# RWKV-5 attention with a two-layer feed-forward: three transposes given to transposing DMAs

## The chip, the core and the metric

The kernel runs on one core of one Trainium2 chip. The metric is the device time in microseconds (us). Before the change it is 203.04 us, the median of three runs (202.64 to 203.18). A profile is one execution of the program, recorded by the hardware profiler.

## What is computed

The reference first runs a recurrent attention over 4 batches, 8 heads, 768 time steps and a head width of 48, and then a feed-forward on its output:

```python
for t in range(S):
    cur = einsum('bhd,bhe->bhde', u * k[t], v[t])
    y[t] = einsum('bhd,bhde->bhe', r[t], state + cur)
    state = w * state + einsum('bhd,bhe->bhde', k[t], v[t])
x = y.transpose(0, 2, 1, 3).reshape(B * S, H * D)       # 3072 x 384
h = x @ w_in                                            # 384 x 2048
g = where(h >= 1, h, where(h <= -1, 0, (h + 1) ** 2 / 4))
out = g @ w_out                                         # 2048 x 384
```

Inputs and output are float32.

## The kernel before

The recurrence is cut into 6 chunks of 128 time steps. Inside a chunk it becomes matmuls: R and K are scaled by powers of w that depend on the row (tiles `Rs` and `Ks`, bf16), the scaled products of all pairs of steps form a 128 x 128 matrix A per head, a mask keeps the earlier steps, and the chunk's sum over K and V updates a state per batch.

A *unit* is one chunk of one batch (128 rows, all 8 heads); a *group* is two units, that is one chunk of two batches. There are 12 groups (0 to 11) and 24 units. Heads are taken in pairs: each head's 48 columns are padded to 64, so a pair fills 128 columns, and a unit has NP = 4 pairs.

For a unit, the stages are these functions:

- `att0` (lines 214 to 224): eight TensorE transposes (tile `T` in PSUM, line 221), four of the unit's scaled R and four of its scaled K, and one VectorE copy to `TT` in SBUF (line 223).
- `att1` (226 to 236): eight matmuls for A from `TT` (line 232), masked by VectorE into `AT` (line 235, two instructions).
- `att2` (238 to 272): `Sp`, the state's sum, from the untransposed `Ks` and V (line 247); `Y` from `TT` with the state (line 254) and from `AT` with V (line 259); VectorE forms `Tm` (266) or the first state (269), and `y` (271), to which it adds the term with u, `V2`.
- `att3` (287 to 295): three TensorE transposes of `y` (tile `X`, line 292).
- `att4` (297 to 299): a ScalarE copy of `X` into half of `xT`, the group's input to the feed-forward.
- `decay` (GpSimd, line 279) and `new_state` (ScalarE, line 285) bring the state forward.

For a group, `load_rk` (lines 77 to 80) issues one DMA for R and one for K on the SP queue, and `load_v` (84) one for V on GpSimd's queue. Both have 48-element runs, 192 bytes in DRAM. `product` (180 to 197) has four GpSimd multiplications: 0 makes `Rs` (line 191), 1 makes `Ks` (193), 2 `KU` (195), 3 `RKU` (197). `u_sums` (VectorE, line 201, tile `diag`) sums RKU, and `u_term` (GpSimd, line 206) makes `V2`. For group 0 the work is split by unit, and VectorE makes its `Rs` and `Ks`. There are three buffers each for R, K, `Rs` and `Ks`, five for V and two for y.

The feed-forward of a group has four quarters. `mm1` (310) is 12 matmuls into `hp` (PSUM, two buffers); `act` is two ScalarE instructions, `pt` (321) and `sq` (323); `act_end` is one VectorE instruction, `gt` (329). `mm2` (341) takes eight of the 16 matmuls of a unit's output into `op` (PSUM, one buffer); after the second half ScalarE copies `op` to `o_sb` (347, two buffers) and SP stores it (349).

The order is written out by hand: every engine and every DMA queue takes its instructions in the order in which the program names them, and an instruction that waits holds up all behind it on its engine. The loop over steps t, four steps per group, is what sets that order. Which stage falls in which step comes from the offsets in these lines:

```python
at_a, at_b, at_1, at_2, at_p = at(0), at(2), at(L1), at(L2), at(-4)   # L1, L2 = 7, 11
at_e = at(L1 + 1)
```

So for group g: `att0` and `att1` of its two units at steps 4g to 4g+3; `att2` and `att3` (with `att4`) at 4g+2 to 4g+5; `mm1` at 4g+7 to 4g+10; `act_end` one step later; `mm2` at 4g+11 to 4g+14; the four products at 4g-4 to 4g-1. Inside a step the order is: `att0` or `att1`; the loads of R and K of the group two ahead (in steps that divide by four, from step 4 on) and of V; `act_end`; `mm1` and `act`; `att2` or `att3`; the product; `u_sums` and `u_term`; `mm2` with its store. R and K of groups 0, 1 and 2 are issued ahead of the loop. The weights `w_in` (two DMAs, line 93, ahead of the loop) and `w_out` (two DMAs, line 97, step 3) are loaded on GpSimd's queue.

Of the kernel before, what the change touches and what calls it, by code (L numbers as in the profile page):

```python
# [9 lines left out]
BF16 = mybir.dt.bfloat16  # L10
# [4 lines left out]
P = 128  # L15
# [3 lines left out]
UNITS = 2  # L19
# [3 lines left out]
def kernel(  # L23
# [11 lines left out]
    nc = tc.nc  # L35
    B, H, S, D = r.shape
    NCH = S // C
    NP = H // 2
# [3 lines left out]
    nK = DM // P  # L42
# [10 lines left out]
    att = ctx.enter_context(tc.tile_pool(name="att", bufs=2))  # L53
# [3 lines left out]
    ps1 = ctx.enter_context(tc.tile_pool(name="ps1", bufs=1, space=bass.MemoryType.PSUM))  # L57
# [8 lines left out]
    def load_tiles(g):  # L66
        R = loads.tile([P, UNITS * H, D], F32, name="R", tag="R")
        K = loads.tile([P, UNITS * H, D], F32, name="K", tag="K")
        V = loads.tile([P, UNITS * H, D], BF16, name="V", tag="V", bufs=5)
        loaded[g] = (R, K, V)  # L70
# [6 lines left out]
    def load_rk(g, j0=0, j1=UNITS):  # L77
        R, K, V = loaded[g]
        nc.sync.dma_start(out=R[:, j0 * H : j1 * H, :], in_=source(r, g, j0, j1))  # L79
        nc.sync.dma_start(out=K[:, j0 * H : j1 * H, :], in_=source(k, g, j0, j1))  # L80

    def load_v(g, j0=0, j1=UNITS):
        V = loaded[g][2]
        nc.gpsimd.dma_start(out=V[:, j0 * H : j1 * H, :], in_=source(v, g, j0, j1))  # L84
# [33 lines left out]
    for j in range(UNITS):  # L118
# [13 lines left out]
    ident = const.tile([P, P], BF16, name="ident")  # L132
# [4 lines left out]
        out=umask, in_=umask, compare_op=ALU.is_ge, fill=1.0,  # L137
# [12 lines left out]
    states_bf = [const.tile([P, NP, 2 * D], BF16, name="state_bf", tag=f"sb{b}") for b in range(B)]  # L150
# [9 lines left out]
    for j in range(2):  # L160
        rows = slice(j * HP, j * HP + D)
# [8 lines left out]
    ready = {}  # L170
# [9 lines left out]
    def product(g, i, eng=None, j0=0, j1=UNITS):  # L180
        eng = eng or nc.gpsimd
        R, K, V, R_s, K_s, KU, RKU, diag, V2 = ready[g]

        def part(x):
            return x.rearrange("p (b h) d -> p b h d", b=UNITS)[:, j0:j1]

        def rep(x):
            return x.unsqueeze(1).to_broadcast([P, j1 - j0, H, D])

        if i == 0:  # L190
            eng.tensor_mul(part(R_s)[:, :, :, :D], part(R), rep(Wup))  # L191
        elif i == 1:
            eng.tensor_mul(part(K_s)[:, :, :, :D], part(K), rep(Wdn))  # L193
        elif i == 2:
            eng.tensor_mul(part(KU), part(K), rep(u_row))  # L195
        else:
            eng.tensor_mul(part(RKU), part(R), part(KU))  # L197

    def u_sums(g, j0=0, j1=UNITS):
        hs = slice(j0 * H, j1 * H)  # L200
        nc.vector.tensor_reduce(ready[g][7][:, hs], ready[g][6][:, hs, :], AX.X, ALU.add)  # L201

    def u_term(g, eng, j0=0, j1=UNITS):
        hs = slice(j0 * H, j1 * H)
        V, diag, V2 = ready[g][2], ready[g][7], ready[g][8]
        eng.tensor_mul(  # L206
            V2[:, hs, :], V[:, hs, :], diag[:, hs].unsqueeze(2).to_broadcast([P, (j1 - j0) * H, D])
        )


    unit = {}
    xT = {}

    def att0(n):
        g, j = divmod(n, UNITS)
        R_s, K_s = ready[g][3:5]
        T = ps1.tile([P, 2 * NP, P], BF16, name="T", tag="a")
        for i, x in enumerate((R_s, K_s)):
            for p in range(NP):
                h = j * H + 2 * p  # L220
                nc.tensor.transpose(T[:, i * NP + p, :], x[:, h : h + 2, :].rearrange("p h d -> p (h d)"), ident)  # L221
        TT = att.tile([P, 2 * NP, P], BF16, name="TT", tag="TT")
        nc.vector.tensor_copy(TT, T)  # L223
        unit[n] = [TT, None, None]

    def att1(n):
        TT = unit[n][0]
        A2 = [ps1.tile([P, NP, P], F32, name=f"A{j}", tag="ab"[j]) for j in range(2)]
        for p in range(NP):
            for j in range(2):  # L230
                rows = slice(j * HP, j * HP + D)
                nc.tensor.matmul(A2[j][:, p, :], TT[rows, NP + p, :], TT[rows, p, :], start=True, stop=True)  # L232
        AT = att.tile([P, 2, NP, P], BF16, name="AT", tag="AT")
        for j in range(2):
            nc.vector.tensor_mul(AT[:, j], A2[j], umask.unsqueeze(1).to_broadcast([P, NP, P]))  # L235
        unit[n][1] = AT

    def att2(n):
        g, j = divmod(n, UNITS)
        c, b = g // BP, (g % BP) * UNITS + j  # L240
        V, K_s, V2 = ready[g][2], ready[g][4], ready[g][8]
        TT, AT, _ = unit[n]
        if c + 1 < NCH:
            Sp = ps1.tile([P, NP, 2 * D], F32, name="Sp", tag="b")
            for p in range(NP):
                h = j * H + 2 * p
                nc.tensor.matmul(  # L247
                    Sp[:, p, :], K_s[:, h : h + 2, :].rearrange("p h d -> p (h d)"),
                    V[:, h : h + 2, :].rearrange("p h d -> p (h d)"), start=True, stop=True,
                )  # L250
        Y = ps1.tile([P, H, D], F32, name="Y", tag="y")
        for p in range(NP):
            if c:
                nc.tensor.matmul(  # L254
                    Y[:, 2 * p : 2 * p + 2, :].rearrange("p h d -> p (h d)"), TT[:, p, :], states_bf[b][:, p, :],
                    start=True, stop=False, skip_group_check=True,
                )
            for i in range(2):
                nc.tensor.matmul(  # L259
                    Y[:, 2 * p + i, :], AT[:, i, p, :], V[:, j * H + 2 * p + i, :],  # L260
                    start=(c == 0), stop=True, skip_group_check=True,
                )
        if c + 1 < NCH:
            if c:
                Tm = att.tile([P, NP, 2 * D], F32, name="Tm", tag="Tm")
                nc.vector.tensor_add(Tm, Sp, states[b])
                decays[n] = Tm
            else:
                nc.vector.tensor_mul(states[b], Sp, wCm)
        y = att.tile([P, DM], BF16, name="y", tag="y")  # L270
        nc.vector.tensor_add(y, Y.rearrange("p h d -> p (h d)"), V2[:, j * H : (j + 1) * H, :].rearrange("p h d -> p (h d)"))
        unit[n][2] = y
# [14 lines left out]
    def att3(n):  # L287
        g, j = divmod(n, UNITS)
        y = unit.pop(n)[2]
        X = ps1.tile([P, nK, P], BF16, name="X", tag="y")  # L290
        for i in range(nK):
            nc.tensor.transpose(X[:, i, :], y[:, i * P : (i + 1) * P], ident)  # L292
        if j == 0:
            xT[g] = moe.tile([P, nK, TOK], BF16, name="xT", tag="xT", bufs=3)
        unit[n] = X

    def att4(n):
        g, j = divmod(n, UNITS)
        nc.scalar.copy(xT[g][:, :, j * P : (j + 1) * P], unit.pop(n))  # L299


    gs = {}
# [76 lines left out]
    for t in range(N):  # L379
        for n, odd in [(g * UNITS + i // 2, i % 2) for g, i in at_a.get(t, ())]:  # L380
            att1(n) if odd else att0(n)
            if n == 0:
                if odd:
                    u_sums(0, 0, 1)
                    u_term(0, nc.vector, 0, 1)
                else:
                    product(0, 0, nc.vector, 1, 2)
                    product(0, 1, nc.vector, 1, 2)
        if t % nQ == 0 and 3 <= t // nQ + 2 < nG:
            g = t // nQ + 2  # L390
            load_tiles(g)
            load_rk(g)
        if t % nQ == 1 and t // nQ + 2 < nG:
            load_v(t // nQ + 2)
        if t == 3:
            load_w_out(0)
            load_w_out(1)
        for g, q in at_e.get(t, ()):
            act_end(g, q)
        for g, q in at_1.get(t, ()):  # L400
            mm1(g, q)
            act(g, q)
        for n, odd in [(g * UNITS + i // 2, i % 2) for g, i in at_b.get(t, ())]:
            att3(n) if odd else att2(n)
            if odd:
                att4(n)
                decay(n)
            elif n:
                new_state(n - 1)
        if t == 2:  # L410
            u_sums(0, 1, 2)
            u_term(0, nc.vector, 1, 2)
        for g, i in at_p.get(t, ()):
            if g:
                if i == 0:
                    prepare_tiles(g)
                product(g, i)
        if t % nQ == 0 and 0 < t // nQ < nG:
            u_sums(t // nQ)
            u_term(t // nQ, nc.gpsimd)  # L420
        for g, i in at_2.get(t, ()):
            mm2(g, i)
# [30 lines left out]
```

## Time and profile before

| | |
|---|---|
| median of three runs | 203.04 us |
| the profiled execution | 203.65 us |
| its span, first to last instruction | 201.9 us |
| busy: TensorE, VectorE, ScalarE, GpSimd | 171.6, 140.3, 140.5, 134.3 us |
| granted TensorE clock | 1.00 throughout |
| T on TensorE (line 221), 192 matmuls | 10.3 + 10.5 us |
| TT on VectorE (line 223), 24 copies | 16.6 us, 690 ns each |
| X on TensorE (line 292), 72 matmuls | 8.5 us |
| xT on ScalarE (line 299), 24 copies | 11.0 us, 460 ns each |
| SP queue (R, K, u, out) | 53168 packets, 14.36 MB, 34.6% of 16 engines |
| GpSimd queue (V, weights, w) | 27712 packets, 5.51 MB, 31.4% |

How to read it. The profile gives, for each engine, the time in which it was busy, and the span in 40 slices in which a digit is the busy share in tenths. Its *chain of waits* starts at the last instruction and goes back, at each step, to what released it; a line's share of that chain says how much of the span it held up. Groups of instructions are named by source line, engine, and what they write and read; "hp<-xT,w_in_sb" is the matmul that writes `hp`. Matmuls overlap in the pipeline, so the mean of one (278 ns for `mm1`) is longer than the distance between two; the chain shows the latter. "SPq" is the SP engine's issuing of DMAs; how long after its issue a transfer has landed is shown apart from that. SP's instructions are not counted as busy.

### The profile page before, as it was taken

What the parts mean: (1) busy time and instruction counts of PE and PEld (TensorE: products, weight loads), DVE (VectorE), ACT (ScalarE), POOL (GpSimd) and SP (SyncE); (2) the same over time, 40 slices, a digit from 0 to 9 for tenths busy, and PEclk for the clock granted to TensorE, in tenths of its full rate; (3) what the DMA queues carried; (4) which work ended last, traced back from release to release, by engine and by line L of the source; (5) the groups of instructions that cost most, each with busy time, mean ns of one, the idle gap of its engine ahead of it and who ended that gap; (6) DMA issues with size and microseconds to landing.
All of it is one profiled execution on the core that took longest, in us unless ns stands there. A gap on an engine that the chain in (4) does not pass through costs nothing.

```text
span 201.9 us, 4347 instructions
## 1 busy us (share of the span) xinstructions
PE 171.6 (85%) x1768; PEld 129.3 (64%) x1768; DVE 140.3 (70%) x197; ACT 140.5 (70%) x173; POOL 134.3 (67%) x102
## 2 busy tenths in 40 slices
PE   0045419979999999999999999999999999999782
PEld 0023317767778777877787778777877786777541
DVE  3189636598968888869688888697787876543320
ACT  4511010789887878787878787878788878898810
POOL 7079999989798796996996969969969020000000
PEclk9999999999999999999999999999999999999999
DMA  5999999999978278836873785568110111101121
GB/s 110 171 212 187 202 135 172 182 158 174 173 45 177 63 64 171 77 82 128 67 152 85 42 196 65 76 136 81 39 40 4 39 42 39 42 0 41 39 78 42
DMA packets 81044, 20.34 MB, mean 101 GB/s; under 512 B 74880, under 2 KB 80256, under 8 KB 81024
## 3 DMA queue, kind: packets, MB, share of 16 engines
q1 hardware_dynamic: 53168, 14.36, 34.6%
q0 software_dynamic: 27712, 5.51, 31.4%
q8 instruction: 14, 0.23, 0.5%
q10 hardware_dynamic: 144, 0.20, 0.5%
q14 instruction: 6, 0.05, 0.1%
HBM read 20.84 MB, written 4.72 MB: 127 GB/s over the span
## 4 chain that ended last, share of the span: by engine, by line
PE 75%; POOL 8%; DVE 4%; DMA 3%; ACT 3%; issue 3%; SPq 2%; POOLq 0%; ACTq 0%
PE hp L310 31%; PE op L341 29%; PE T L221 5%; PE A L232 3%; DMA u_bc<-in_u_dram 3%; PE Y L259 2%; POOL KU L195 2%; PE X L292 2%; POOL RKU L197 2%; PE Y L254 2%; ACT pt L321 2%; SPq L79 2%; PE Sp L247 1%; ACT o_sb L347 1%; POOL V L84 1%
## 5 line engine op out<-in xcount | busy, mean ns | idle before, releaser
L321 ACT ACTIVATE pt<-hp,half_col 128x1024 f32<-128x1024 f32 x48 | 53.4, 1113 | 31.6 <-PE hp L310 31.3
L310 PE MATMUL hp<-xT,w_in_sb 128*128 128x256 bf16 x576 | 72.9, 278 | 1.1 <-DVE gt L329 1.1
L341 PE MATMUL op<-w_out_sb,gt 128*128 128x384 bf16 x384 | 69.9, 326 | 2.3 <-ACT o_sb L347 2.0
L329 DVE SCALAR_TENSOR_TENSOR gt<-sq,hp 128x1024 bf16<-128x1024 f32 x48 | 58.2, 1213 | 12.5 <-ACT sq L323 12.5
L310 PEld LDWEIGHTS <-w_in_sb 128*128 128x128 bf16 x576 | 54.8, 99 | 10.7 <-issue 1.4
L323 ACT ACTIVATE sq<-pt,zero_col 128x1024 f32<-128x1024 f32 x48 | 55.2, 1149 | 1.6
L341 PEld LDWEIGHTS <-gt 128*128 128x128 bf16 x384 | 35.2, 97 | 22.3 <-issue 3.1
L235 DVE TENSOR_TENSOR AT<-A,umask 128x512 bf16<-128x512 f32 x48 | 30.8, 683 | 7.4 <-PE A L232 7.2
L223 DVE COPY TT<-T 128x1024 bf16<-128x1024 bf16 x24 | 16.6, 690 | 21.8 <-PE T L221 21.8
L206 POOL TENSOR_TENSOR V<-V,diag 128x768 f32<-128x768 bf16 x11 | 16.2, 1474 | 20.6 <-DVE diag L201 20.3
L221 PE MATMUL T<-ident,Rs 128*128 128x128 bf16 x96 | 10.3, 237 | 18.7 <-DVE Rs L191 10.1
L195 POOL TENSOR_TENSOR KU<-K,u_bc 128x768 f32<-128x768 f32 (+1 forms) x13 | 22.0, 1689 | 6.4 <-DMA u_bc<-in_u_dram 6.4
L197 POOL TENSOR_TENSOR RKU<-R,KU 128x768 f32<-128x768 f32 (+1 forms) x13 | 22.1, 1700 | 0.3
L221 PEld LDWEIGHTS <-Rs 128*128 128x128 bf16 x96 | 8.0, 106 | 21.6 <-DVE Rs L191 10.6
L299 ACT COPY xT<-X 128x384 bf16<-128x384 bf16 x24 | 11.0, 460 | 14.3 <-PE X L292 14.3
L193 POOL TENSOR_TENSOR Ks<-K,Wdn 128x768 bf16<-128x768 f32 x11 | 20.0, 1817 | 0.0
L191 POOL TENSOR_TENSOR Rs<-R,Wup 128x768 bf16<-128x768 f32 x11 | 19.9, 1813 | 0.0
L279 POOL TENSOR_TENSOR state<-Tm,wCm 128x384 f32<-128x384 f32 x16 | 16.0, 1002 | 0.1
L347 ACT COPY o_sb<-op 128x384 f32<-128x384 f32 x24 | 11.2, 467 | 5.7 <-PE op L341 5.7
L232 PE MATMUL A<-TT 48*128 48x128 bf16 x192 | 11.6, 232 | 3.4 <-DVE TT L223 2.0
L84 POOL DMA_DIRECT2D V<-in_v_dram x12 | 14.4, 1202 | 0.0
L201 DVE TENSOR_REDUCE diag<-RKU 128x16 f32<-128x768 f32 (+1 forms) x13 | 11.5, 881 | 3.1 <-POOL RKU L197 3.1
(48 smaller groups left out, 145.8 us busy)
## 6 DMA issues: line engine op xcount, KB each, us to landing
out_dram<-o_sb SPq DMA_DIRECT2D x24, 192.0 KB, 1.9
R<-in_r_dram SPq DMA_DIRECT2D x11, 384.0 KB, 4.4
K<-in_k_dram SPq DMA_DIRECT2D x11, 384.0 KB, 6.0
V<-in_v_dram POOLq DMA_DIRECT2D x12, 192.0 KB, 5.0
w_in_sb<-in_moe_w_in_dram POOLq DMA_DIRECT2D x2, 768.0 KB, 9.0
w_out_sb<-in_moe_w_out_dram POOLq DMA_DIRECT2D x2, 768.0 KB, 17.1
R<-in_r_dram SPq DMA_DIRECT2D x2, 192.0 KB, 6.0
K<-in_k_dram SPq DMA_DIRECT2D x2, 192.0 KB, 5.4
```

The source lines that it names most:

```text
L191: eng.tensor_mul(part(R_s)[:, :, :, :D], part(R), rep(Wup))
L193: eng.tensor_mul(part(K_s)[:, :, :, :D], part(K), rep(Wdn))
L195: eng.tensor_mul(part(KU), part(K), rep(u_row))
L197: eng.tensor_mul(part(RKU), part(R), part(KU))
L221: nc.tensor.transpose(T[:, i * NP + p, :], x[:, h : h + 2, :].rearrange("p h d -> p (h d)"), ident)
L232: nc.tensor.matmul(A2[j][:, p, :], TT[rows, NP + p, :], TT[rows, p, :], start=True, stop=True)
L235: nc.vector.tensor_mul(AT[:, j], A2[j], umask.unsqueeze(1).to_broadcast([P, NP, P]))
L310: nc.tensor.matmul(hp[:, f, :], w_in_sb[:, i, n0 : n0 + P], xT[g][:, i, :], start=(i == 0), stop=(i == nK - 1), skip_group_check=True,)
L321: nc.scalar.activation(pt, hp, AF.Relu, bias=half_col, scale=0.5)
L323: nc.scalar.activation(sq, pt, AF.Square, bias=zero_col)
L329: nc.vector.scalar_tensor_tensor(out=gt, in0=sq, scalar=1.0, in1=hp, op0=ALU.min, op1=ALU.max)
L341: nc.tensor.matmul(o_ps[g], gs[g, q][:, f, j * P : (j + 1) * P], w_out_sb[:, n, :], start=(n == 0), stop=(n == nF - 1),)
```

## The change

All transposes but those of group 0's R and K leave TensorE. A new function, `transpose_in`, issues one transposing DMA on SP for a group's whole `Rs` (128 x 1024) or `Ks`, right behind the product that makes it, in the steps 4g-4 and 4g-3. Its result, `RT` or `KT`, has three buffers. `att0` is left with nothing to issue for groups 1 to 11, and takes the unit's half of these tiles. `att3` issues one transposing DMA on SP for a unit's y (128 x 384), straight into its half of `xT`, and `att4` is gone, with the ScalarE copy. In `att1` and `att2`, `TT[0]` is the transposed R and `TT[1]` the transposed K.

```diff
+    scaled_T = {}
+
+    def transpose_in(g, i):
+        x = ready[g][3 + i].rearrange("p h d -> p (h d)")
+        t = att.tile([P, UNITS * NP, P], BF16, name="TT"[:1] + "RK"[i], tag="RK"[i] + "T", bufs=3)
+        nc.sync.dma_start_transpose(out=t, in_=x)
+        scaled_T[g, i] = t
+
     def att0(n):
         g, j = divmod(n, UNITS)
+        if g:
+            cols = slice(j * NP, (j + 1) * NP)
+            unit[n] = [[scaled_T[g, i][:, cols, :] for i in range(2)], None, None]
+            return
...
-        unit[n] = [TT, None, None]
+        unit[n] = [[TT[:, :NP, :], TT[:, NP:, :]], None, None]
...
-                nc.tensor.matmul(A2[j][:, p, :], TT[rows, NP + p, :], TT[rows, p, :], start=True, stop=True)
+                nc.tensor.matmul(A2[j][:, p, :], TT[1][rows, p, :], TT[0][rows, p, :], start=True, stop=True)
...
     def att3(n):
         g, j = divmod(n, UNITS)
         y = unit.pop(n)[2]
-        X = ps1.tile([P, nK, P], BF16, name="X", tag="y")
-        for i in range(nK):
-            nc.tensor.transpose(X[:, i, :], y[:, i * P : (i + 1) * P], ident)
         if j == 0:
             xT[g] = moe.tile([P, nK, TOK], BF16, name="xT", tag="xT", bufs=3)
-        unit[n] = X
-
-    def att4(n):
-        g, j = divmod(n, UNITS)
-        nc.scalar.copy(xT[g][:, :, j * P : (j + 1) * P], unit.pop(n))
+        nc.sync.dma_start_transpose(out=xT[g][:, :, j * P : (j + 1) * P], in_=y)
...
             if odd:
-                att4(n)
                 decay(n)
...
                 product(g, i)
+                if i < 2:
+                    transpose_in(g, i)
```

More of the change, by code (lines that the diff above doesn't have):

```diff
@@ L254, in att2 @@
                 nc.tensor.matmul(
-                    Y[:, 2 * p : 2 * p + 2, :].rearrange("p h d -> p (h d)"), TT[:, p, :], states_bf[b][:, p, :],
+                    Y[:, 2 * p : 2 * p + 2, :].rearrange("p h d -> p (h d)"), TT[0][:, p, :], states_bf[b][:, p, :],
                     start=True, stop=False, skip_group_check=True,
```

## The prediction

> **What bounds the kernel now.** I read the page's slices and chain first, then the chain in order of time in the middle, then the SP queue's timeline at the start.
>
> ```profile
> PE   0045419979999999999999999999999999999782
> ...
> DMA  5999999999978278836873785568110111101121
> ...
> PE hp L310 31%; PE op L341 29%; PE T L221 5%; PE A L232 3%; DMA u_bc<-in_u_dram 3%; PE Y L259 2%; POOL KU L195 2%; PE X L292 2%; POOL RKU L197 2%; PE Y L254 2%; ACT pt L321 2%; SPq L79 2%; PE Sp L247 1%; ACT o_sb L347 1%; POOL V L84 1%
> ```
>
> A slice is 5.05 us. There are three stages. To about 45 us TensorE is idle or half busy, while the DMA row reads 9 up to 60 us. From 45 to 171 us TensorE is full. After 171 us TensorE and ScalarE take turns. The chain's T (5%) and X (2%) are the transposes that the change takes away. The middle of the chain, in order of time (start, us, what):
>
> ```profile
> 97.23 1.31 PE hp L310 x12
> 98.54 0.17 PE Sp L247 x4
> ...
> 99.08 1.30 PE op L341 x8
> 100.38 0.33 PE A L232 x8
> 100.71 1.42 PE hp L310 x12
> 102.12 0.17 PE X L292 x3
> 102.29 1.30 PE op L341 x8
> 103.59 0.45 PE T L221 x8
> 104.04 1.31 PE hp L310 x12
> ```
>
> Two steps of the loop take 6.81 us (97.23 to 104.04) without a gap, and all of it is TensorE. The SP queue at the start (start, us in the queue's issue):
>
> ```profile
> 12.74 1.49 SPq L80 DMA_DIRECT2D K<-in_k_dram  x1
> 16.59 1.97 SPq L79 DMA_DIRECT2D R<-in_r_dram  x1
> 18.66 9.11 SPq L80 DMA_DIRECT2D K<-in_k_dram  x1
> 28.67 5.18 SPq L79 DMA_DIRECT2D R<-in_r_dram  x1
> 33.94 9.40 SPq L80 DMA_DIRECT2D K<-in_k_dram  x1
> 43.43 4.23 SPq L79 DMA_DIRECT2D R<-in_r_dram  x1
> 47.71 4.43 SPq L80 DMA_DIRECT2D K<-in_k_dram  x1
> 53.99 0.36 SPq L349 DMA_DIRECT2D out_dram<-o_sb  x1
> ```
>
> These are K of group 2, R and K of groups 3, 4, 5, and the first store. By the tile view of K and R in narrow windows, K2 lands 14.9 us after its issue (at 27.6), R3 15.5 (32.1), K3 24.7 (43.4), R4 19.2 (47.9), K4 18.0 (51.9). An issue's end coincides with a landing: K3's with K2's (27.8, 27.6), K4's with K3's (43.3, 43.4), R5's with R4's (47.7, 47.9). So SP gets about two loads ahead and then waits for the oldest, and the loads land in the order of issue. The start is bound by this queue.
>
> **The middle: what is removed.** T is 0.45 us every second step; it lies on the chain from 49.10 to 164.55, so 18 times: 8.1 us. X is 0.17 us in each other step from 47.63 on, 20 times: 3.4 us. Together 11.5 us, and two steps become 6.19 us. What is late next: VectorE needs per two steps 2 x 1.21 (gt) + 2 x 0.68 (AT) + 0.55 (y) + 0.55 (Tm) + half of 0.94 (diag) = 5.4 us (the 0.69 of TT goes); ScalarE 2 x 2.26 + 0.47 + 0.50 = 5.5 us (the 0.46 of xT goes); GpSimd per four steps 4 x 1.81 + 1.47 + 1.20 + 2 x 1.00 = 11.9 against 12.4 us. All still fit. Closest is the hp buffer, of which there are two: hp started at 97.06, its gt ended at 103.16 behind AT, so the hp two steps later can't start before 6.15 to 6.2 us. That may take back 0 to 1 us; I take 11.0 for the middle.
>
> **The middle: what is added.** Per group SP issues two transposes of 128x1024 and two of 128x384, and each waits in SP's order for its source. No DMA of this kind is in the trace. *SP's time for it*: between 0.36 us (an unhindered store) and the 1.41 us that K's issue has as its median; I take 1 to 1.5, as it has half of a load's pieces but is another instruction. That makes 4 to 6 us, beside 1.8 for the loads and 0.7 for the stores, of 12.4. *The engines' time*: a load is 2048 pieces of 192 B; a transpose reads 1024 (384 for y) rows of 256 B. In the undisturbed middle K lands 1.55 us behind R (R's landing 3.9 us, K's 5.0, issued 0.45 later), 0.76 ns a piece. At that price a group's 2816 rows take 2.1 us; the nearest lower bound is nothing, the upper one I set at twice the price per row. The DMA share was 0.68 between 60 and 100 us, 9.3 us in a group of 13.62; 9.3 + 2.1 to 4.2 us against 12.4 may meet the bound of one full set of engines, but shares up to 1.58 are in the trace (40 to 50 us), so I cost it at nothing.
>
> The 128x1024 results have cover: Rs is ready in the step of its product (105.88 in the group around 104) and read five steps later; Ks ends at 113.19 and is read three to four steps later. For y: the late half is ready at 106.83; SP is held by the store until 108.84; with 1 us of issue and some 2 to 3 us to land (a store takes 1.9) it is there at 112, and the hp that reads it starts two steps on, at 114.3. The cover is 2 us; if a y transpose took 5.5 us, each further us would cost one per group, 11 in all. Behind a transpose that waits on SP stand only stores and loads: o_sb has two buffers and two steps a store (6 us), the loads are four steps ahead.
>
> The Trainium skill speaks against the change here. "VectorE: DVE Perf Modes", section The three transpose paths, gives 1309 ns for a 128x128 transpose by DMA and 390 ns on TensorE, and its rules say to use TensorE where PSUM will do. Eight T took 0.45 us in this trace, 56 ns each, so the page's TensorE figure isn't what this kernel pays. By the page's DMA figure, an estimate, 22 blocks a group would take 29 us and the kernel some 190 us more. [...]
>
> **The start: what is moved.** Here I expect the change to lose. SP's order becomes: ... K2; R' and K' of group 1 (steps 0, 1; a dash marks a transpose); y' of unit 0 (step 3); R3, K3 (step 4); R'2 (step 4, behind the loads in the code); y' of unit 1 (step 5). The first mm1 needs both y' and started at 33.05. Now SP waits for Rs of group 1 (GpSimd, ends 20.32) and for Ks (23.28), so R3's issue moves from 16.59 to about 26, and y' of unit 1 stands behind K3, which landed at 43.4 even when it was issued early.
>
> The queue from K2's landing at 27.6 holds, up to that y': 1024 + 1024 + 384 + 2048 (R3) + 2048 (K3) + 1024 + 384 = 7936 rows or pieces. R3 and K3 together landed in 15.8 us (27.6 to 43.4), 260 a us, beside w_out, whose second half lands at 45.2 (25.9 + 19.3); afterwards R4 and K4 landed in 8.5 us, 480 a us. So 17.6 us x 260 = 4580 by 45.2, and the other 3360 in 7.0 us: 52.2. The V load of step 5 is gone at 48.9 (32.2 + 16.7), after which it is faster: 50.3 if the last 1500 go at 0.76 ns. I take **51** for the first mm1. Ends: 44 if the transposes cost the queue nothing, 60 if a row costs twice a piece.
>
> From the first mm1 to the first mm2 it was 33.1 to 47.8, 14.7 us, a stretch set by VectorE (gt, AT, diag one behind the other); one TT of 0.6 us goes: 14.1. Nothing there catches up: GpSimd's u_term waits for diag, which stands behind the first gt. Then 201.9 - 47.8 = 154.1 us, less 11.0. The tail keeps its turns: the last xT copy ended at 178.36; y is ready at 173.75 and 4 us by DMA gives the same. Sum: 51 + 14.1 + 143.1 = 208.2 us of span, 6.3 above 201.9. The execution took 203.65, 1.75 above its span and 0.6 above the median of 203.04. On the median: 203.04 + 6.3 = **209.3 us**.
>
> **Rivals.**
> - *The start loses more than the middle gains* (forecast): first mm1 between 46 and 60, 204 to 218 us. Chance 0.55.
> - *Transposes nearly free for the queue*: first mm1 at 44 to 46, 201.5 to 204. For it: no HBM is read. Against: loads ahead remain. 0.13.
> - *The transposes do not stand behind the loads' pieces* (the faster side): another path lets y' of unit 1 pass R3 and K3. SP still issues it behind K3, whose issue would end when K2 has landed (27.8), then R'2 after Rs at 30.4, y' at about 31.5, landed by 34 to 36. The middle's 11 us remain: 191.5 to 196. It decides as soon as y' lands before 44. For it: loads and weights on two queues did pass each other. Against: SP's own loads land strictly in order. 0.19.
> - *Slow transposes*: above about 3.7 ns a row (five times a piece) a group's 10.4 us and the other 9.3 pass 1.58 x 12.4, and the engines bind the middle; at twice that, about 19 us a group for some 8 groups, 55 us more. 218 to 270. For it: a transpose splits its rows over 128 partitions, and no row shows its price. 0.13.
>
> **Numbers.** About 0.3% (0.6 us) can be told from no change. Faster: 0.19 and 0.05 of the second; same 0.05; slower 0.71. The range reaches from the upper end of the third rival to the cheaper half of the last: 196.5 to 225.
>
> **What would show it.** Right: in the SP queue R3 issued at 24 to 28 us and y' of unit 1 behind K3; the first hp (L310) at 46 to 60; two steps in the middle of 6.2 us with no T and X; no wait of hp for xT there. Wrong: hp starting by 36; repeated idle of TensorE before hp in the middle (y' slower than its 5.5 us); a DMA row of 9 to the end; SP issues of several us for a transpose.

## The result

The changed kernel takes 216.38 us, the median of four runs (214.77 to 216.82), against 203.06 us before: 1.0645 times as long, with a 95% interval of 1.0588 to 1.0702. The profiled execution has a span of 214.5 us against 201.9.

So it is slower, as forecast, but by 13.3 us and not by 6.3. The loss at the start came as forecast: the first hp was put at 51 us and started at 50.65. The gain behind it did not: it was put at 11.6 us and is 5.0.

### The profile page after: what moved, and what is told of

The parts are those of the page before. It is cut to its first block, busy times and chain, and to the rows that moved or that the text cites. A ratio compares the mean times of both kernels' runs of the same rounds, so it can differ in the third digit from the quotient of the medians.

```text
span 214.5 us, 3905 instructions
## 1 busy us (share of the span) xinstructions
PE 157.3 (73%) x1520; PEld 114.1 (53%) x1520; DVE 127.2 (59%) x175; ACT 131.7 (61%) x149; POOL 134.3 (63%) x102
## 2 busy tenths in 40 slices
DMA packets 114258, 28.44 MB, mean 133 GB/s; under 512 B 108096, under 2 KB 113472, under 8 KB 114240
## 4 chain that ended last, share of the span: by engine, by line
PE 30%; DVE 17%; DMA 16%; ACT 12%; POOL 11%; issue 7%; SPq 4%; DVEq 0%; POOLq 0%; ACTq 0%
PE hp L315 16%; PE op L346 11%; DMA R<-in_r_dram 7%; ACT pt L326 6%; DMA xT<-y 6%; DVE gt L334 6%; ACT sq L328 5%; DVE diag L201 4%; DVE AT L247 3%; DMA u_bc<-in_u_dram 3%; POOL KU L195 3%; POOL Rs L191 3%; DVE Tm L278 2%; DVE y L283 2%; POOL V L84 2%
## 5 line engine op out<-in xcount | busy, mean ns | idle before, releaser
L315 PEld LDWEIGHTS <-w_in_sb 128*128 128x128 bf16 x576 | 55.7, 100 | 34.5 <-issue 19.8
L346 PEld LDWEIGHTS <-gt 128*128 128x128 bf16 x384 | 36.0, 97 | 22.7 <-issue 3.1
L244 PE MATMUL A<-TR,TK 48*128 48x128 bf16 x176 | 9.8, 226 | 11.7 <-DMA TK<-Ks 10.4
L297 ACT CAST state_bf<-state 128x384 bf16<-128x384 f32 x20 | 9.9, 497 | 12.2 <-DVE state L281 12.2
L244 PEld LDWEIGHTS <-TK 48*128 48x128 bf16 x176 | 5.4, 97 | 18.1 <-DMA TK<-Ks 10.5
L283 DVE TENSOR_TENSOR y<-Y,V 128x384 bf16<-128x384 f32 x24 | 13.1, 547 | 0.0
L271 PE MATMUL Y<-V,AT 128*128 128x48 bf16 x192 | 11.7, 188 | 0.0
```

The lines of the kernel that those rows point to most:

```text
L315: nc.tensor.matmul(hp[:, f, :], w_in_sb[:, i, n0 : n0 + P], xT[g][:, i, :], start=(i == 0), stop=(i == nK - 1), skip_group_check=True,)
L346: nc.tensor.matmul(o_ps[g], gs[g, q][:, f, j * P : (j + 1) * P], w_out_sb[:, n, :], start=(n == 0), stop=(n == nF - 1),)
```

## The profile after

The page's slices and its chain of waits, by line:

```profile
PE   0142104005769999999899999969999999999873
...
DMA  6999999999778989979899797998954311211111
...
PE hp L315 16%; PE op L346 11%; DMA R<-in_r_dram 7%; ACT pt L326 6%; DMA xT<-y 6%; DVE gt L334 6%; ACT sq L328 5%; DVE diag L201 4%; DVE AT L247 3%; DMA u_bc<-in_u_dram 3%; POOL KU L195 3%; POOL Rs L191 3%; DVE Tm L278 2%; DVE y L283 2%; POOL V L84 2%
```

A slice is now 5.36 us. TensorE reads 4 or less in the first nine, up to 48.3 us, and 9 for the first time in the thirteenth (64.4 us); before, it read 9 from the seventh on (30.3 us). The first hp waits for y' of unit 1 (a dash marks a transpose):

```profile
50.65 0.37 PE L315 MATMUL hp<-xT,w_in_sb 128*128 128x256 bf16 x1 [13.72 <-DMA xT<-y]
```

In brackets stands the engine's idle time before the instruction, and what ended it. T and X are gone from the chain, but the chain is no longer TensorE's: two DMAs (R's load and xT) and VectorE's gt, diag, AT, Tm and y have come in. The SP queue at the start (start, us of issue):

```profile
20.25 4.02 SPq L219 DMA_TRANSPOSE TR<-Rs  x1
24.38 3.49 SPq L219 DMA_TRANSPOSE TK<-Ks  x1
27.96 1.22 SPq L304 DMA_TRANSPOSE xT<-y  x1
29.23 0.59 SPq L79 DMA_DIRECT2D R<-in_r_dram  x1
29.88 4.25 SPq L80 DMA_DIRECT2D K<-in_k_dram  x1
34.24 12.78 SPq L219 DMA_TRANSPOSE TR<-Rs  x1
47.11 1.20 SPq L304 DMA_TRANSPOSE xT<-y  x1
```

R3 is issued at 29.23 where it was 16.59, because SP waits for GpSimd's Rs first, to 20.25, and then is busy with the issue of three transposes. The second TR spends 12.78 us in its issue, to 47.02; R3 had landed 2.3 us earlier, at 44.71, 15.5 us after its own issue. y' of unit 1 is issued at 47.11 and lands 3.5 us later, and hp starts at 50.65.

The next table follows the first hp of some groups (g is the group) and the span's end, in us, from the timelines:

| | g 0 | g 1 | g 3 | g 6 | g 9 | end |
|---|---|---|---|---|---|---|
| before | 33.05 | 46.15 | 73.40 | 114.26 | 154.96 | 201.9 |
| after | 50.65 | 63.72 | 89.74 | 129.07 | 169.07 | 214.5 |
| difference | 17.60 | 17.57 | 16.34 | 14.81 | 14.11 | 12.6 |

Group 5 to 6 takes 12.81 us, where 12.4 was reckoned. Its four gaps between hp starts are 2.62, 3.58, 3.04 and 3.57; before they were 3.24, 3.57, 3.24 and 3.57. The first gap gave the full 0.62 us of a T and an X, the third only 0.20. The chain in order of time through the second half of that group shows why:

```profile
116.32 1.43 PE hp L315 x12
...
117.78 1.12 ACT pt L326
...
118.92 1.16 ACT sq L328
...
120.11 0.46 DVE gt L334
...
121.25 0.55 DVE Tm L278
121.80 0.47 DVE y L283
122.26 0.86 DVE diag L201
123.12 0.88 DVE AT L247 x2
...
124.23 1.22 DVE gt L334
...
125.50 1.47 PE hp L315 x12
```

The hp at 125.50 waits for the gt of 124.23, which frees its buffer. That gt stands on VectorE behind Tm, y, diag and AT in one unbroken row. There is one diag in a group, so this happens once in a group. Three groups were held up otherwise as well. The waits of TensorE between 60 and 175 us (waiter, what it waited for: us in total, times, longest):

```profile
PE hp L315 <- DVE gt L334: 3.9, 9, 1.9
...
PE hp L315 <- DMA xT<-y: 2.8, 3, 1.7
```

And SP's queue ahead of the y' that the longest wait for xT was for:

```profile
131.85 0.57 SPq L79 DMA_DIRECT2D R<-in_r_dram  x1
132.47 2.40 SPq L80 DMA_DIRECT2D K<-in_k_dram  x1
134.99 2.35 SPq L219 DMA_TRANSPOSE TR<-Rs  x1
137.44 0.52 SPq L354 DMA_DIRECT2D out_dram<-o_sb  x1
138.05 1.20 SPq L304 DMA_TRANSPOSE xT<-y  x1
```

Two things make this y' late. It was ready at 135.07 and stood 3.0 us behind R' and a store in SP's order, and then it took 5.52 us to land instead of the median 2.3. R' and the store ahead of it had landed by 139.62, 1.6 us after its issue. Beside it ran a load of V from the other queue, issued at 137.43. The y' of the second unit of groups 2 to 7 stand behind the same K, R' and store, and R' lands 1.1 to 1.2 us after the issue of y' in all six; what differs is how long before y' the load of V was issued (us, from the timelines and landings):

| group | 2 | 3 | 4 | 5 | 6 | 7 |
|---|---|---|---|---|---|---|
| V issued before y' by | 0.43 | -0.15 | 0.64 | 0.10 | 0.25 | 0.62 |
| y' landed after its issue | 4.37 | 2.60 | 4.67 | 3.76 | 4.01 | 5.52 |
| hp then waited | 0.33 | 0 | 0.83 | 0 | 0 | 1.68 |

So the trace puts the long landing on V's load. No run moved that load to test it, and it does not cover every case: with R and K back on TensorE (below) one y' took 5.62 us with V's load issued 0.25 us behind it, and one 4.31 us with none beside it.

## The experiments

The kernels before and after have 203 and 216.4 us; all runs stand beside runs of the kernel before on the same chip. First the start: which of its parts makes y' or A late?

**y back on TensorE**, R and K by DMA.

```diff
-        nc.sync.dma_start_transpose(out=xT[g][:, :, j * P : (j + 1) * P], in_=y)
+        X = ps1.tile([P, nK, P], BF16, name="X", tag="y")
+        for i in range(nK):
+            nc.tensor.transpose(X[:, i, :], y[:, i * P : (i + 1) * P], ident)
+        nc.scalar.copy(xT[g][:, :, j * P : (j + 1) * P], X)
```

> R and K by transposing DMAs as in the changed kernel, y transposed on TensorE as before. Place theory (the start is lost because transposes stand in SP's one queue behind the loads of group 3, whatever they carry): the first hp needs no y' any more and starts at 36 to 38 us (after the first K' lands at 33), but R' and K' of group 2 still stand behind R3 and K3, so TensorE then waits for A of unit 4 until about 50 us; 207 to 212 us in all. Rival (only the late y' of unit 1 sets the start): first hp at 33 to 37, nothing else late, 196 to 200 us.

212.09 us, 1.045 times the kernel before (1.041 to 1.048). The first hp started at 36.53, and then:

```profile
53.18 0.61 PE L244 MATMUL A<-TR,TK 48*128 48x128 bf16 x8 [10.94 <-DMA TK<-Ks]
```

A of unit 4 came at 53.18 after a wait of 10.94 us for K' of group 2. That K' stood in SP's order behind R' of group 2, which was issued at 32.59 behind K3, spent 13.56 us in its issue and landed 18.0 us after it began; K' could only be issued at 46.24. Taking y away frees the first hp, but the next transpose behind the same loads holds TensorE instead. The rival falls. From group 1 on the gaps were 2.79, 3.57, 2.87 and 3.57 us: 12.81 a group with X still on TensorE.

**R and K back on TensorE**, y by DMA: `att0` works for all groups as it did, and `transpose_in` is not called.

```diff
-        if g:
-            cols = slice(j * NP, (j + 1) * NP)
-            unit[n] = [[scaled_T[g, i][:, cols, :] for i in range(2)], None, None]
-            return
...
-                if i < 2:
-                    transpose_in(g, i)
```

> R and K transposed on TensorE as before, y by transposing DMAs. Place theory: R3 is issued at about 20 us, K3 behind it, and y' of unit 1 lands behind K3, as K3 landed at 43.4 in the kernel before: first hp at 44 to 46 us, a loss of 11 to 13, of which the missing X give back 3: 210 to 214 us. Rival (the transposes' own weight in the full queue delays the start): only 768 rows are left of it ahead of the first hp, first hp by 36 us, 199 to 204 us.

213.96 us (1.053, 1.049 to 1.058); first hp at 45.77. SP's queue:

```profile
23.69 6.03 SPq L80 DMA_DIRECT2D K<-in_k_dram  x1
29.81 10.30 SPq L304 DMA_TRANSPOSE xT<-y  x2
```

K3 landed 20.8 us after its issue, at 44.5, and y' of unit 1 15.8 us after its own, at 45.6. Two y' of 384 rows cost 12.7 us, nearly all of it by their place: y' of unit 1 landed 1.1 us behind K3. The rival, that it is the transposes' own weight, falls for this kernel.

**The loads of group 3 behind y'.** 

```diff
-            load_rk(g)
+            if g > 3:
+                load_rk(g)
...
+        if t == 5:
+            load_rk(3)
```

> As the changed kernel, but R and K of group 3 are issued at the end of step 5, behind the transposes of R and K of group 2 and of y of unit 1; every transpose is still there. Place theory: y' of unit 1 lands at about 38 us, first hp at 37 to 40; R3 and K3 land at 45 to 52, which GpSimd just bears: 203 to 207 us. Rival (the transposes' own weight): first hp still above 45 us, 212 to 217 us.

214.60 us (1.057, 1.055 to 1.059): a miss. The chain in order of time has two waits for a y':

```profile
31.63 11.21 DMA xT<-y
...
42.98 2.73 PE hp L315 x12
...
55.79 4.34 DMA xT<-y
...
60.18 1.89 PE hp L315 x8
```

y' of unit 1, with no load of R or K ahead of it any more, took 11.21 us. Behind K2 (landed at 27.80) stood only transposes, 1024 + 1024 + 384 + 1024 + 384 = 3840 rows, and they were through at 42.84: 255 a us beside w_out, close to the 260 of the forecast. The expected 38 us would have needed some 370. So the transposes' own rows alone hold the first hp back to 43 us, as the place alone held it back to 45.77 in the run before; each is enough, and together they make 50.65. Then y' of unit 3, ready at 57.9 in the changed kernel and at about 50 here, stood behind the loads that now came later. GpSimd also waited 10.8 us for R3. Of 7.7 us won at the first hp, 4.1 were lost again by the first hp of group 1 (60.18 against 63.72), and more afterwards.

**w_out later.**

```diff
-        if t == 3:
+        if t == 7:
             load_w_out(0)
```

> The changed kernel with w_out's two loads issued at step 7 in place of 3, after the first fifth of the span; all transposes and loads of SP in the same order. If the start is set by SP's queue sharing the engines with the weights (some 180 rows a us beside w_out, 450 without): the first hp at 43 to 47 us in place of 50.65, 208 to 213 us. If only the order counts, or the transposes themselves are slow: the first hp at 49 to 52, 215 to 218 us.

214.70 us (1.056, 1.051 to 1.061). The first hp came at 42.06, earlier than any theory had it: R3 landed 7.25 us after its issue in place of 15.5, so the weights do slow SP's queue. But A of unit 4 then waited for K' until 50.27, while w_out was being loaded, and the first hp of group 1 started at 59.51. In time at most 2 us are won, and the interval overlaps that of the changed kernel (1.0588 to 1.0702). Removing one late transfer showed the next one.

**Plain copies in the place of the transposes.** The issue reads, for R and K (y likewise; the pad of 16 columns keeps the runs at 256 B):

```diff
-        x = ready[g][3 + i].rearrange("p h d -> p (h d)")
-        t = att.tile([P, UNITS * NP, P], BF16, name="TT"[:1] + "RK"[i], tag="RK"[i] + "T", bufs=3)
-        nc.sync.dma_start_transpose(out=t, in_=x)
+        x = ready[g][3 + i].rearrange("p h d -> p (h d)").rearrange("p (k c) -> p k c", k=UNITS * NP)
+        t = att.tile([P, UNITS * NP, P + 16], BF16, name="TT"[:1] + "RK"[i], tag="RK"[i] + "T", bufs=3)
+        nc.sync.dma_start(out=t[:, :, :P], in_=x)
```

> Every transposing DMA replaced, at the same place of SP's order, by a plain copy of the same tile in runs of 256 B (1024 and 384 rows); the computation then takes untransposed data, all other work is the same. Order and row count theory (the place in the one queue and the number of rows, not the transposing): first hp at 48 to 52 us, 213 to 218 us. Rival (the transposing itself is slow beside the loads): first hp at 43 to 47, 205 to 212 us.

214.28 us (1.055, 1.052 to 1.059). The first hp started at 50.70, against 50.65 with transposes. The start does not care whether the DMA transposes; the rival falls there. In the middle the copies do better: no hp waits for xT once group 1 has started. SP's issue of a copied y takes 0.60 us in the median, that of a transposed y 1.19, but y is held on SP for about as long as before (1.8 to 2.7 us in groups 3 to 8). What differs is the landing beside a load of V: with that load issued 0.30 us ahead a copied y took 2.92 us, and a transposed one 4.01 at 0.25 us. By these rows the transposing itself costs time there; why is open.

**Copies of R and K in rows of 2 KB**, without the pad.

```diff
-        t = att.tile([P, UNITS * NP, P + 16], BF16, name="TT"[:1] + "RK"[i], tag="RK"[i] + "T", bufs=3)
+        t = att.tile([P, UNITS * NP, P], BF16, name="TT"[:1] + "RK"[i], tag="RK"[i] + "T", bufs=3)
```

> As the kernel with plain copies, but R and K are copied in rows of 2 KB (128 rows in place of 1024), y still in 384 runs of 256 B. If the count of rows sets their weight in the full queue: the loads of group 3 and y of unit 1 land earlier, first hp at 44 to 47 us, 3 to 7 us below the kernel with 256 B runs. If bytes count, or the place alone: first hp at 48 to 52 as there.

209.64 us (1.033, 1.031 to 1.035), 4.6 less. The first hp at 47.04 is 3.7 us earlier, with the same 28.44 MB in 93810 packets in place of 113522. So the number of rows counts. What is left of the loss at the first hp, 14 us, is mainly the place: y' of unit 1 still stands behind K3, which landed at 45.09, and came in at 47.00.

**From group 4 on.** Groups 0 to 3 stay on TensorE (in `att3` too, with X and its copy as above), so that no transpose stands in the full queue.

```diff
-        if g:
+        if g >= 4:
             cols = slice(j * NP, (j + 1) * NP)
...
-                if i < 2:
+                if i < 2 and g >= 4:
                     transpose_in(g, i)
...
+        if g >= 4:
+            nc.sync.dma_start_transpose(out=xT[g][:, :, j * P : (j + 1) * P], in_=y)
+            return
```

> Groups 0 to 3 as in the kernel before (TensorE transposes all), transposing DMAs from group 4 on. The start is as before: first hp at 33 us by all theories. For the middle: tie theory (hp has two buffers, and in the pair of steps with diag the gt that frees one comes late): a group takes 12.8 us where the DMAs are used, some 0.8 us less than 13.62, for 7 or 8 groups, less 2 to 3 us of waits for xT: 197 to 201 us. Rival (the transposing DMAs load the engines so that nothing is gained in the middle): 202 to 206 us.

198.21 us, 0.974 of the kernel before (0.970 to 0.979). The start is untouched (first hp 33.44), groups take 12.81 us where nothing waits, and two hp waited for xT, 1.3 us together. It is faster than both kernels.

Now the middle: what keeps a group at 12.8?

**No transposes at all.**

```diff
     def transpose_in(g, i):
+        return
...
-            unit[n] = [[scaled_T[g, i][:, cols, :] for i in range(2)], None, None]
+            unit[n] = [first_T[j], None, None]
...
     def att3(n):
...
+        if g:
+            xT[g] = xT[0]
+            return
```

Group 0's y is transposed on TensorE and copied by ScalarE, as in the kernel before.

> Left out: every transpose of R and K but group 0's (all later units use group 0's transposed tiles) and every transpose of y but group 0's (all later groups multiply group 0's xT); nothing takes their place. All the rest of the work is done. This is what the removal alone can be worth. Tie theory: groups of 12.81 us, gaps between hp 2.62, 3.57, 3.04, 3.57: 193.5 to 195.5 us. The averaged reckoning of the forecast: groups of 12.4 to 12.5 us, 190.5 to 192.5 us.

194.95 us (0.961, 0.958 to 0.965), gaps 2.62, 3.58, 3.04, 3.57. With no DMA in the way the removal is worth 8 us and no more; the third gap is there without any transpose to wait for. The hp behind it waits for gt:

```profile
92.63 1.47 PE L320 MATMUL hp<-xT,w_in_sb 128*128 128x256 bf16 x12 [0.26 <-DVE gt L339]
```

**The same with diag a step later**, behind gt:

```diff
+        if t % nQ == 1 and 0 < t // nQ < nG:
+            u_sums(t // nQ)
+            u_term(t // nQ, nc.gpsimd)
...
-        if t % nQ == 0 and 0 < t // nQ < nG:
-            u_sums(t // nQ)
-            u_term(t // nQ, nc.gpsimd)
```

> Left out as in the kernel without transposes; diag and u_term a step later, behind gt. Tie theory: the third gap falls from 3.04 to 2.62, 0.42 us in each of some 10 groups: 189 to 191.5 us, at least 3 us below the kernel that leaves diag in its place. If GpSimd (11.9 us of work a group) or something else sets 12.8: no change, 193.5 to 195.5.

191.98 us (0.945, 0.942 to 0.948), gaps 2.62, 3.58, 2.62, 3.58. VectorE's timeline (the last two entries of a line are the tile's form and the wait):

```profile
100.80 1.29 DVE L246 TENSOR_TENSOR AT<-A,umask 128x512 bf16<-128x512 f32 x2 [0.29 <-PE A L243]
102.00 1.21 DVE L339 SCALAR_TENSOR_TENSOR gt<-sq,hp 128x1024 bf16<-128x1024 f32 x1
103.13 0.95 DVE L201 TENSOR_REDUCE diag<-RKU 128x16 f32<-128x768 f32 x1
103.32 1.47 PE L320 MATMUL hp<-xT,w_in_sb 128*128 128x256 bf16 x12
```

gt ends at 103.21 and hp starts at 103.32, with diag beside it. The tie is shown: 3 us, by moving one instruction of VectorE and what hangs on it.

**From group 4 on, y on TensorE throughout.** To the kernel from group 4 on:

```diff
-        if g >= 4:
-            nc.sync.dma_start_transpose(out=xT[g][:, :, j * P : (j + 1) * P], in_=y)
-            return
```

> R and K by transposing DMAs from group 4 on, y on TensorE throughout. Tie theory: the hp buffer sets the group at 12.81 us with or without X, and no hp waits for xT, so this is as good as or better than with y by DMA (198.2): 196 to 198 us. Rival (each X on TensorE is on the path, 0.34 us a group): 199.5 to 202 us.

196.84 us (0.970, 0.967 to 0.973): the lowest time of the kernels that do all the work, though its interval touches that of the kernel from group 4 on with y by DMA (0.970 to 0.979). A group takes 12.81 us again, X included, and no hp waits for xT. The gaps are 2.79, 3.58, 2.87 and 3.57: the fourth hp of a group starts 9.24 us behind the first, as without X (2.62, 3.58 and 3.04). X only fills time that TensorE would otherwise wait, so moving y to a DMA gains nothing here.

**From group 4 on, diag a step later.** The kernel from group 4 on, with the diff of diag shown above.

> As the kernel that uses the DMAs from group 4 on, and diag (u_sums) with its u_term a step later, behind the gt of the step that divides by four plus one. Tie theory: the gt that frees the hp buffer comes 0.9 us earlier, the third gap between two hp falls from 3.04 to about 2.6 us where T and X are gone, 0.4 us a group for 7 to 8 groups: 194 to 196.5 us. Rival (that gap is set by the DMAs' arrival or by TensorE itself): gap unchanged, 197.5 to 199.5 us.

208.38 us (1.028, 1.021 to 1.034). The gap went from 3.04 to 2.62 as the tie theory has it, and the time went up by 10 us all the same: hp waited for xT three times, 10.1 us together. With diag later, V's load is issued ahead of u_term, and GpSimd had no slack left (Rs to Rs 12.53 us against a group of 12.4). The trace shows a part for each. The three y' were held on SP for 4.3 to 4.5 us after they were ready, behind an R' that came late from GpSimd (1.9 to 2.2 for the same groups in the kernel from group 4 on), and then took 5.3 to 5.6 us to land, with V's load issued 2.7 us ahead. Which of the two would be enough wasn't tried. What came behind a wait of 3.46 us, in stretches (from:to, length, busy us of TensorE, its weight loads, VectorE, ScalarE, GpSimd, then the granted clock, the DMA share and GB/s):

```profile
80.00:83.00 3.00, 3.00 (x36) 2.23 (x34) 2.53 (x4) 2.65 (x3) 2.33 (x2) 1.00 1.58 162
83.00:87.00 4.00, 0.54 (x10) 0.30 (x10) 2.62 (x4) 1.41 (x3) 4.00 (x4) 1.00 0.78 137
87.00:90.00 3.00, 3.00 (x15) 1.97 (x16) 0.00 (x0) 0.71 (x1) 3.00 (x3) 0.57 0.64 155
```

After the idle stretch the granted clock is 0.57 and the matmuls of hp take 421 ns in the median in place of 273.

**From group 4 on, loads behind the transposes** of the step after:

```diff
             load_tiles(g)
-            load_rk(g)
...
+        if t % nQ == 1 and 3 <= t // nQ + 2 < nG:
+            load_rk(t // nQ + 2)
         for g, i in at_2.get(t, ()):
```

> As the kernel that uses the DMAs from group 4 on, with all loads of R and K from group 3 on issued behind the transposes of the step after, so that no y' of a group's second unit stands behind fresh loads. If the hp's waits for xT in the middle (0.9 and 0.5 us there) come from the place behind those loads: they go, 196.3 to 197.8 us. If they come from the engines' total load: unchanged, 198 to 199 us. If the loads come too late for GpSimd: GpSimd waits for R, above 200 us.

204.25 us (1.001, 0.997 to 1.005), and the waits for xT grew to 6.0 us. The loads then stood behind the transpose of K, and GpSimd waited 7.5 us for R, as in the third case of the expectation. R' came later, y' stands behind R' in SP's order, and the three late y' were held there for 3.0 to 3.2 us. They then took 5.6 to 5.9 us to land with no load of R or K in flight ahead of them, and with V's load issued 0.6 us ahead. So the place behind the loads of R and K was not what made y' late; y' ahead of R' wasn't tried, nor V's load behind y'.

## Why the forecast was right and wrong

*What bounds the kernel* held: a start set by SP's queue, a middle set by TensorE, a tail that keeps its turns. The page's rows were misread a little: TensorE's reads 9 from 30 us, not from 45, and DMA's reads 9 up to 55 us, not 60. The sum goes by the first hp at 33.05 and does not use this.

*The start* held, step by step. R3's issue moved to 29.2 (26 was reckoned, but SP spent 4.0 and 3.5 us in the issue of the first R' and K'), y' of unit 1 came behind R3 and K3, and the first hp at 50.65 (51). R3 landed at 44.7 (29.23 + 15.5) with 4480 rows and pieces done since K2 landed (27.84), 266 a us (260); of the rest, R' of group 2 came only 0.8 us behind K3 (50.1 and 49.3), so the end was a little faster than reckoned. The price of a row equal to that of a load's piece held: 3840 rows of transposes alone went at 255 a us where the loads had gone at 260. The 0.6 us of a TT less between the first hp and the first mm2 did not come whole: that stretch is 14.39 us, 14.59 before, and 14.17 in the kernel with diag moved.

*The middle's gain* is the step that failed: "That may take back 0 to 1 us; I take 11.0 for the middle." VectorE's load was averaged over steps, "half of 0.94 (diag)", and the hp buffer was checked in the pair of steps at 97.06, which has no diag. In the other pair Tm, y, diag and AT stand ahead of the gt that frees the buffer. By that row the fourth hp of a group starts 9.24 us behind the first, where TensorE alone needs 8.82 (2.62, 3.58 and 2.62 with diag moved). That takes back 0.42 us in each of some nine groups, 3.8 us. From the first hp to the end the changed kernel gains 5.0 us, the kernel without transposes 8.1 (1.2 earlier at the first hp, 9.3 at the end), and the one with diag moved 11.8. The 11.6 of the forecast are there, but only with diag moved as well and no y' to wait for.

*The cover of y'*, "2 us", with 5.5 us as the point where it ends, is the second step that failed. The mechanism was named, but the sum put it at nothing: three groups waited, 0.4, 0.9 and 1.74 us by their gaps, 3.0 in all. The reckoning had "some 2 to 3 us to land" and left out the load of V that is issued about when y' is; beside it y' took 3.8 to 5.5 us. SP held y' 2.2 to 3.0 us in groups 2 to 7, near the 2.0 reckoned. 3.8 and 3.0 are the 6.6 us that are missing, within 0.2.

*The rivals.* No transpose passed the loads' pieces; the transposes were neither free for the queue (45.77 with 768 rows, 50.65 with all) nor slow by themselves: K' lands 3.0 us after its issue in the median, y' 2.3. Only y' beside a load of V was slower than a copy.

## What to carry to other kernels

A DMA that replaces work of an engine enters an in-order queue with everything else that this queue does: ask what stands ahead of it when the queue is full, and start such a change after the stretch in which it is full (here from group 4 on: 2.6% faster, and 3.0% with only R and K moved). When time is taken from the bound engine, check each step of a period for what comes second, not the mean of the period: one instruction in one step of four took back a third of the gain. The median landing of a transfer is not its landing beside a load of another queue that comes at the same point of every period. Moving a load to relieve one waiter showed the next waiter each time; what helped was fewer rows, or no transfer there.

## What was not expected of the hardware

SP's issue of a transpose takes 1.19 us for 128x384 and at the least 1.23 for 128x1024, within the 1 to 1.5 that the forecast took; the surprise is that this is twice the 0.60 us of a plain copy of the same rows. With a full queue it goes up to 12.78 us. For loads, SP gets two ahead, 4096 pieces: in the kernel before, K3's issue ended at 27.77 when K2 landed (27.63), and K4's at 43.34 when K3 landed (43.40). What a transpose takes of this room is not settled: with copies the issue of the second TR ended with R3's landing (42.97 and 43.07), with transposes 2.3 us after it.

The Trainium skill, "Advanced Engine Details and Errata", section X-Bar Transpose (TRN2), has transposing DMAs as fast as regular ones. For the transfer in the full queue, the first hp at 50.65 and 50.70 us agrees; SP's issue time does not, nor does the landing beside a load of V (4.01 us against a copy's 2.92). In "VectorE: DVE Perf Modes", section The three transpose paths, a 128x128 block takes 1309 ns; here eight of them land in 3.0 us together.

A wait of TensorE of 3.46 us was followed by a granted clock of 0.57 for some 3 us, and the gap that followed was 4.29 us in place of 2.62, so this wait cost 1.7 us on top. The wait of 1.7 us in the changed kernel was followed by a gap of 2.62. In the kernel with the loads behind the transposes, a wait of 2.11 us was also followed by 2.62, but one of 2.08 by a granted clock of 0.61 and a gap of 4.29:

```profile
143.00:146.50 3.50, 3.50 (x18) 2.26 (x19) 0.37 (x1) 1.39 (x2) 2.38 (x3) 0.61 1.01 200
```

"TensorE: Matmul & The Clock Gate", section Why this matters for your kernels, puts the limit at about 3 us of idleness. The wait of 3.46 us fits that; the one of 2.08 us shows that a shorter one can be enough. What tells it from the one of 2.11 us is not known.
